# Threshold attention and a squared-ReLU network on one core: earlier loads for the third pair, an own order for attention's last two periods, and the last stores of the hidden layer asked for by ScalarE

## The chip, the core and the metric

One NeuronCore of a Trainium2 chip runs the whole program: TensorE (PE, the matrix engine), VectorE (DVE), ScalarE (ACT), GpSimd (POOL) and SyncE (SP), each with an instruction stream of its own, which it works off in order. The engines meet through semaphores. SP does no arithmetic: it asks for DMA transfers. ACT can ask for transfers too, as one more instruction of its own stream. The metric is the device time of one execution in microseconds (us), lower is better.

## The reference, cut to what matters

```python
# q, k, v: 8 batches x 8 heads x 576 x 64, fp32
scores = scale * np.matmul(q, k.transpose(0, 1, 3, 2))
thresh = np.max(scores, axis=-1, keepdims=True) - tau
scores = np.where(scores >= thresh, scores, -1000000000.0)
scores = scores - np.max(scores, axis=-1, keepdims=True)
attn = np.exp(scores)
attn = attn / (np.sum(attn, axis=-1, keepdims=True) + 1e-09)
attn_out = np.matmul(attn, v)
# to 4608 tokens x 512
x = attn_out.transpose(0, 2, 1, 3).reshape(B * S, H * D)
h = np.maximum(x @ w_in, 0.0)        # w_in 512 x 2048
out = h * h @ w_out                  # w_out 2048 x 512
```

## The kernel before, in words

**Attention** works on 32 pairs of heads. A pair's 2 x 576 query rows are cut into units of 128 rows, and with them the kernel counts unit pairs, 0 to 71 (called m). The work is laid out in periods (72 and a few more to fill and drain the pipeline). Each period runs a list of step names, in `run_period`; a name with `-` behind it belongs to the period before, with `--` to the one before that. There are two general lists (`PLAIN` and `CONVERTING`; the latter with steps that convert a chunk of the weights of `w_in`), and `BEGIN_WITH` holds lists of their own for periods 0 and 1. The order of the names is the order in which each engine gets its instructions.

The steps that matter here:

- `T` turns a pair's queries or keys on PE (transposes, L422) into `sc`, the tile of six PSUM banks.
- `SA`, `SB`, `RA`, `RB` are the score products (L458); `top`, `least`, `pow`, `mask`, `over` and `inv` are the softmax with its threshold, on DVE (L476, L491), POOL (L483) and ACT (L486).
- `V`, `W`, `U` turn the weights of one unit pair on PE (L402): `V` the first four of nine chunks of keys, `W` the fifth, `U` the last four. `V` and `U` write to `pt`, a PSUM place of two banks, which only one of them can hold at a time; `W` writes to banks 2 and 3 of `sc`. `Q` spreads the sums of the rows (L541) into what is left of `W`'s banks.
- `eV`, `eW`, `eU` copy the results to SBUF, by ACT (L549, in `filled`).
- `PV` multiplies the values with the turned weights over nine chunks of keys (L558), into banks 0 and 5; `x` takes the result out by ACT (L689) and DVE (L691), and `xm` scales one half on POOL (L701) and gives it to a store (L604).

Which instruction waits for which is worked out from the tiles; within `sc` the function `touch` tells the scheduler that accesses to different banks do not depend on one another, except for the pairs of kinds that `MEET` names, which do share data through SBUF.

**Loads at the start.** All are asked for by SP, in program order. `load_k` yields the key loads of a pair one by one, and last the two parts of `rn` (the 577th to 640th place of the turning: the last keys, L327, and the last queries, L328). The steps `ahead` and `more` ask for up to five such loads each. `load_v` (L337) loads a pair's values; the main loop calls it after periods 0, 1 and 2 for pairs 0, 1 and 2, and later ones follow when a place comes free. L194 loads chunks of `w_in`, which come as 64-bit numbers and are converted on ACT (L208), POOL and DVE for the hidden layer.

**The hidden layer** multiplies x with `w_in` by a scheme of seven products in place of eight, two levels deep. It runs in passes over blocks of tokens: the last is pass n = 8. In a pass the outer products come in the order `OUTER` = 1, 2, 6, 7, 4, 5, 3 (called m), and in each the inner products in the order 1, 6, 7, 5, 2, 4, 3 (`inner`, matmuls at L799). After inner product 1 ACT copies it from PSUM (L794): `copy(p1, X)`. Product 2 goes on in the same bank, so it needs that copy done. The other sums of a group are made by `final` and `sum_v` on DVE and POOL (L122, L125), some with another copy by ACT (L838).

The results of groups 2, 4, 5 and 3 are squared, four tiles each, by two ACT instructions (L951 and L952, in `square`), six inner products or more later; right behind them SP stores the tile to `g` in DRAM (L955 in pass 8). So pass 8 has 16 such stores of 256 KB.

**The output layer** reads `g` back (L1064) and multiplies it with `w_out` in the same scheme (also L799, the tile then is called `po`), in 9 steps of 49 products of 0.87 us. Its weights were prepared and put to DRAM earlier. In pass 8, while the hidden layer's weights leave `wall` one by one, `reload` (L1207) loads the 49 weights of the output layer into their places, 39 in the pass and 10 in the first output step, all by SP. In SP's order they stand between the stores of L955.

**Transfers.** In the program as built each DMA takes one of eight semaphores, in turn over the whole program and whatever engine asks for it. Before it is asked for, its engine waits until the DMA that took the same semaphore before, eight places back in program order, has landed. That wait stands in the stream of the engine that asks.

Of the kernel before, what the change touches and what calls it, by code (L numbers as in the profile page):

```python
# [48 lines left out]
def kernel(  # L49
# [25 lines left out]
    nc = tc.nc  # L75
# [5 lines left out]
    FULL = S // P  # L81
# [3 lines left out]
    BANK = 512  # L85
    MAIN = FULL * P
    STEP = 512
    NSTEP = B * S // STEP
# [202 lines left out]
    NU = len(units)  # L291
# [80 lines left out]
    behind = mybir.DependencyInfo(mybir.DependencyClass.Sync, mybir.DependencyReason.DATA)  # L372

    Q_RING, K_RING, W_RING = 3, 4, 2
    MEET = (("scores", "turnedq", (Q_RING,)), ("scores", "turnedk", (K_RING,)), ("last scores", "turnedk", (K_RING,)), ("values", "weights", (W_RING,)), ("x", "weights", (W_RING,)))

    def touch(what, made, at, size, key=0):

# [26 lines left out]
    def whole(pt, slot, count):  # L405

        return pt[:, :, ds(slot * HALF, count * HALF)].rearrange("p r (t q) -> p r t q", q=HALF)

    def joined(to):

        return to.rearrange("p (t r q) -> p r t q", r=2, q=HALF)
# [111 lines left out]
    def fill(m, f, pt, at=None):  # L523

        first, count = FILLS[f]
        if m not in wT:
            wT[m] = sb.tile([P, (2 * CH + 2) * P], FP32, tag="wT", bufs=W_RING, name="wT")
        for i, (u, c) in enumerate(FIRST[first : first + count]):
            half_turn(pt, i, weights[2 * m + u][:, c, :, :].rearrange("p j d -> p (j d)"), at)
# [11 lines left out]
                    made = nc.tensor.matmul(to, wide, ident[rows, rows], start=True, stop=True)  # L541
                    touch("turns", made, at + r * BANK, BANK)

    def filled(m, f, pt, at=None):

        first, count = FILLS[f]
        count += 2 * (f == "W")
        to = wT[m][:, ds(weight_at(first) * P, count * P)]
        touch("weights", nc.scalar.copy(joined(to), whole(pt, 0, count)), at, 2 * BANK, m)  # L549

    def values(m):

        for c in range(CH):
            for u in range(2):
                for s, (i, _, count, row) in enumerate(halves(2 * m + u)):
                    for j in range(2):
                        rows = ds(j * D, D)
                        made = nc.tensor.matmul(  # L558
                            sc[ds(u * D, D), ds(5 * j * BANK + row, count)], loaded_v[i][rows, (c - (u != j)) % CH, :],
                            wT[m][rows, ds(weight_at(2 * c + u) * P + row, count)],  # L560
                            start=(c == 0 and s == 0), stop=(c == CH - 1), skip_group_check=True,
                        )
                        touch("values", made, 5 * j * BANK, BANK, m)

    def valued(m):

# [18 lines left out]
    def has(n):  # L585
        return 0 <= n < NU
# [5 lines left out]
    def sums_due(p):  # L592

        return p > max(starts) + 2 and not converts(p)
# [43 lines left out]
        """.split(),  # L638
    }

    def spots():
        return [(sc[:, ds(b * BANK + REST, (FULL + 1) * HALF)], b * BANK) for b in (1, 4)]

    def middle():
        return sc[:, 2 * BANK : 4 * BANK].rearrange("p (r n) -> p r n", r=2)

    def period(p):

# [2 lines left out]
        late, pt = {"W": []}, {}  # L651

        def fills(f, m):
            if has(2 * m):
                pt[f] = pt_pool.tile([P, 2, BANK], FP32, tag="pt", name="pt")
                fill(m, f, pt[f])

        def evict(f, m):
            if has(2 * m):
                filled(m, f, pt[f], 2 * BANK if f == "W" else None)  # L660

        def W():
            if has(2 * m + 2):
                pt["W"] = middle()
                fill(m + 1, "W", pt["W"], 2 * BANK)

        def Q():
            if has(2 * m + 2):
                spread_sums(m + 1, pt["W"], 2 * BANK)

        def turn_some():
            free = None
# [42 lines left out]
        def every(key):  # L715
# [10 lines left out]
            "c1": lambda: convert1(begun(p)), "c2": lambda: convert2(begun(p)),  # L726
            "c3": lambda: convert3(begun(p)), "c4": lambda: convert4(begun(p - 1)),
            "c5": lambda: convert5(begun(p - 1)), "c6": lambda: convert6(begun(p - 1)),
            "s1": lambda: sums_due(p) and sums_step(), "s2": lambda: sums_due(p) and p < 60 and sums_step(), "ahead": lambda: ahead(5), "more": lambda: ahead(5),
            "fetch": lambda: (fetch(begun(p + 2)), fetch(begun(p + 3)) if p > 1 else None), "put": put, "give": lambda: ask(False),  # L730
        }
        steps["over"] = lambda: do(a, "over")
# [216 lines left out]
    def square(n, j, o):  # L949

        nc.scalar.activation(out=o, in_=o, func=AF.Relu)  # L951
        nc.scalar.activation(out=o, in_=o, func=AF.Square)  # L952
        steps, h = n
        if h is None:
            nc.sync.dma_start(out=gT[steps[0]][j][:, :].rearrange("p (k t) -> p k t", k=4), in_=o)  # L955
            return
        for s_, step in enumerate(steps):
            nc.sync.dma_start(
                out=gT[step][j][:, ds(h * BANK // 2, BANK // 2)].rearrange("p (k t) -> p k t", k=2),
                in_=o.rearrange("p (k s) t -> p k s t", s=2)[:, :, s_, :],  # L960
            )
# [199 lines left out]
    with tc.manual_schedule():  # L1161
        with ExitStack() as stack:
# [24 lines left out]
            turn(0, 1, spots(), nc.vector.tensor_copy)()  # L1187
            for p in range(FIRST_PERIOD, NU // 2 + 6):
                run_period(p)
                if 0 <= p < 3:  # L1190
                    load_v(p)
                if X_FIRST <= p < X_FIRST + 4:
                    load_x(0, XPARTS[p - X_FIRST :][:1])
                if p == X_FIRST + 4:
                    summing.append(prepare_x(0, lambda op, out, x, y: op(nc.gpsimd, out, x, y)))
# [191 lines left out]
```

## Time and profile before

| | us |
|---|---|
| time, median of 3 runs | 1281.78 (1280.94 to 1283.04) |
| the profiled execution | 1281.21 |
| its span in the trace | 1279.1 |
| PE busy | 1252.5 (98%) |
| DVE busy | 987.5 (77%) |
| POOL busy | 982.4 (77%) |
| ACT busy | 845.6 (66%) |

The profile is of one execution. Attention takes it to about 495.9 us from its start, the hidden layer to about 883.0, the output layer the rest. The granted clock of PE is nearly full over the whole span. A row of the waits says which engine and operation stood, what it waited for, and then the sum in us, how often, and the longest. A row of the timeline gives start and length in us, engine, line, operation, output and inputs, and in brackets how long the engine stood before and what ended that.

### The profile page before, as it was taken

The numbers are of one execution on the slowest core, as the hardware profiler recorded it, in microseconds if no ns is written. First come the engines' busy times: TensorE is split into PE (matmuls) and PEld (weight loads), VectorE is DVE, ScalarE is ACT, GpSimd is POOL, SyncE is SP. The second block draws the span as 40 slices with busy tenths as digits, with TensorE's granted clock in tenths as the row PEclk, the third lists the DMA queues.
The fourth block names the chain that finished last, engine by engine and source line by source line (L and its number), as shares of the span: only waits on it lengthen the run. The fifth ranks groups of instructions, "written<-read, shape, count | busy, mean of one in ns | idle before, by whom it ended". The sixth has DMA issues, their size and how long they took to land.

```text
span 1279.1 us, 55422 instructions
## 1 busy us (share of the span) xinstructions
PE 1252.5 (98%) x22991; PEld 1093.8 (86%) x22991; DVE 987.5 (77%) x2384; ACT 845.6 (66%) x1537; POOL 982.4 (77%) x1070
## 2 busy tenths in 40 slices
PE   7999999999999999999999999999999999999998
PEld 5777777777777778988888888999999999999998
DVE  6999999999999995886887877876646654665563
ACT  6999999999999994665765857665424432433240
POOL 2899898877776542987897989858777877787776
PEclk9999999999999999999999999999999999999999
DMA  7566667434333323658767868589654235523511
GB/s 185 131 170 149 176 191 195 117 93 104 85 86 86 80 58 84 203 170 232 209 190 215 229 169 239 164 304 361 240 164 162 65 109 167 167 57 112 167 35 35
DMA packets 291450, 196.81 MB, mean 154 GB/s; under 512 B 100096, under 2 KB 252160, under 8 KB 291200
## 3 DMA queue, kind: packets, MB, share of 16 engines
q1 hardware_dynamic: 289888, 192.87, 52.6%
q8 instruction: 181, 2.97, 1.0%
q14 instruction: 69, 0.57, 0.2%
q10 hardware_dynamic: 1312, 0.41, 0.1%
HBM read 120.85 MB, written 72.35 MB: 151 GB/s over the span
## 4 chain that ended last, share of the span: by engine, by line
PE 74%; DMA 2%; DVE 2%; ACT 1%; issue 1%; SPq 0%; POOL 0%; DVEq 0%; POOLq 0%; ACTq 0%
PE po L799 27%; PE ph L982 18%; PE ph L799 10%; PE sc L558 7%; PE sc L458 6%; PE pt L402 4%; PE sc L541 1%; PE sc L422 1%; DVE arena L125 1%; DMA arena<-g 1%; ACT c L838 1%; PE sc L402 0%; DMA wall<-w 0%; DVE arena L122 0%; ACT arena L951 0%
## 5 line engine op out<-in xcount | busy, mean ns | idle before, releaser
L125 POOL TENSOR_TENSOR arena<-arena 128x512 f32<-128x512 f32 (+1 forms) x314 | 378.3, 1224 | 130.5 <-DVE arena L125 118.7
L799 PE MATMUL po<-wall,arena 128*64 128x128 f32 x7056 | 388.3, 273 | 4.2 <-ACT arena L794 2.8
L799 PEld LDWEIGHTS po<-wall,arena 128*64 128x64 f32 x7056 | 386.7, 137 | 5.6 <-ACT arena L794 3.8
L125 DVE TENSOR_TENSOR arena<-ph,arena 128x512 f32<-128x512 f32 x378 | 254.8, 689 | 79.9 <-PE ph L982 31.9
L122 POOL TENSOR_TENSOR arena<-arena 128x128 f32<-128x128 f32 (+1 forms) x322 | 265.6, 826 | 23.8 <-DMA arena<-w 8.2
L982 PE MATMUL ph<-arena,wall 128*128 128x256 f32 x1176 | 256.6, 380 | 1.6 <-DVE arena L125 1.3
L982 PEld LDWEIGHTS ph<-arena,wall 128*128 128x128 f32 x1176 | 222.1, 190 | 36.0 <-DVE arena L125 5.8
L125 DVE TENSOR_TENSOR arena<-po,arena 128x128 f32<-128x128 f32 x378 | 108.0, 289 | 160.6 <-PE po L799 156.8
L491 DVE SCALAR_TENSOR_TENSOR arena<-arena 128x576 f32<-128x576 f32 x288 | 226.0, 821 | 0.0
L486 ACT ACTIVATE arena<-arena 128x576 f32<-128x576 f32 x288 | 213.3, 778 | 13.2 <-DVE arena L476 13.1
L476 DVE TENSOR_SCALAR_CACHE_REDUCE arena<-sc 128x576 f32<-128x576 f32 x288 | 203.3, 753 | 18.8 <-issue 7.7
L838 ACT COPY c<-arena 128x512 f32<-128x512 f32 (+1 forms) x295 | 169.0, 578 | 72.9 <-DVE arena L122 35.5
L458 PE MATMUL sc<-arena 64*64 64x512 f32 (+1 forms) x2304 | 178.8, 415 | 5.6 <-ACT arena L549 1.0
L558 PE MATMUL sc<-arena 64*64 64x128 f32 (+1 forms) x5760 | 165.9, 261 | 1.3 <-ACT arena L549 0.8
L122 DVE TENSOR_TENSOR arena<-arena,c 128x512 f32<-128x512 f32 x235 | 154.4, 666 | 12.7 <-ACT c L838 8.3
L558 PEld LDWEIGHTS sc<-arena 64*64 64x64 f32 x5760 | 150.7, 133 | 4.9 <-issue 1.0
L549 ACT COPY arena<-pt 128x1024 f32<-128x1024 f32 x144 | 145.7, 1012 | 3.8 <-PE pt L402 3.2
L458 PEld LDWEIGHTS sc<-arena 64*64 64x64 f32 x2304 | 76.7, 134 | 70.8 <-issue 46.5
L794 ACT COPY arena<-po 128x128 f32<-128x128 f32 x63 | 16.6, 263 | 181.8 <-PE po L799 177.0
L799 PE MATMUL ph<-arena,wall 128*64 128x128 f32 x2352 | 129.2, 273 | 0.6 <-DVE arena L691 0.6
L799 PEld LDWEIGHTS ph<-arena,wall 128*64 128x64 f32 x2352 | 128.3, 137 | 1.4 <-issue 1.0
L483 POOL TENSOR_SCALAR arena<-arena,tau_p 128x2 f32<-128x2 f32 x144 | 83.7, 581 | 57.9 <-DVE arena L476 43.5
(54 smaller groups left out, 1139.6 us busy)
## 6 DMA issues: line engine op xcount, KB each, us to landing
arena<-g SPq DMA_DIRECT2D x144, 256.0 KB, 5.1
g<-arena SPq DMA_DIRECT2D x192, 128.0 KB, 2.9
w<-arena SPq DMA_DIRECT2D x60, 256.0 KB, 3.0
wall<-w SPq DMA_DIRECT2D x49, 256.0 KB, 5.5
g<-arena SPq DMA_DIRECT2D x48, 256.0 KB, 3.7
arena<-w SPq DMA_DIRECT2D x44, 256.0 KB, 3.4
arena<-in_v_dram SPq DMA_DIRECT2D x32, 288.0 KB, 3.8
out_dram<-arena SPq DMA_DIRECT2D x70, 128.0 KB, 2.9
```

What stands on the lines that cost most here:

```text
L122: e.tensor_tensor(out=out, in0=x, in1=y, op=ALU.subtract)
L125: e.tensor_tensor(out=out, in0=x, in1=y, op=ALU.add)
L458: made = nc.tensor.matmul(sc[at, ds(to, count)], lhs, kT[rows, ds(at_k, count)], start=True, stop=True)
L476: made = nc.vector.tensor_scalar(out=s[:, j, :], in0=sc[:, ds(at, S)], scalar1=1.0, scalar2=None, op0=ALU.mult, op1=ALU.min, accum_out=nmx ...
L483: nc.gpsimd.tensor_scalar(out=thr, in0=nmx, scalar1=tau_p[:, :], scalar2=None, op0=ALU.add)
L486: nc.scalar.activation(out=w[:, :, j, :], in_=of(j), func=AF.Exp, bias=nmx[:, j : j + 1], scale=-1.0)
L491: nc.vector.scalar_tensor_tensor(out=w[:, :, j, :], in0=of(j), scalar=thr[:, j : j + 1], in1=w[:, :, j, :], op0=ALU.is_le, op1=ALU.mult, a ...
L549: touch("weights", nc.scalar.copy(joined(to), whole(pt, 0, count)), at, 2 * BANK, m)
L558: made = nc.tensor.matmul(sc[ds(u * D, D), ds(5 * j * BANK + row, count)], loaded_v[i][rows, (c - (u != j)) % CH, :], wT[m][rows, ds(weigh ...
L799: nc.tensor.matmul(to[cols], lhs[:, cols], rhs, start=start, stop=stop, skip_group_check=True)
L838: nc.scalar.copy(c, y)
L982: nc.tensor.matmul(to[:, 2 * j : 2 * j + 2, :], W_IN[m, k][:, ts(2 * h + j, P)], part_x(steps, k, m), start=(not more and j == 0), stop=Tr ...
```

## The change

It has three parts.

**A.** `load_v` is called after periods 0, 2 and 3 (for pairs 0, 1, 2 as before), and the step `more` asks for up to seven loads of keys and queries instead of five. On SP the two parts of `rn` of the third pair so come directly behind its keys, ahead of the second pair's values and of two chunks of `w_in`.

**B.** Period 73, the last but one that has work, gets its own list, which holds the steps of what is left of both last periods. On PE the values of unit pair 70 now stand before `V` of unit pair 71, where they stood behind it. For unit pair 71 `W` is put into banks 1 and 2, `U` into banks 3 and 4 of `sc` and not into `pt`, and `U` is copied out by DVE instead of ACT. Its values product is told as three kinds, so that only the last four chunks wait for `U`'s copy. POOL's order does not change.

**C.** The 16 stores of pass 8 (`steps[0] == NSTEP - 1`) are asked for by ACT, each right behind its second squaring instruction. SP then has 49 reloads in a row. In ACT's stream from the group m = 5 on stand, in order: copy of product 1 (m = 5), square and store four times, copy of product 1 (m = 3), and then squares and stores with copies of L838 between. (In program order the first of these four stores comes eight places behind the 22nd reload, the second behind the 25th, the third behind the 29th.)

```diff
--- before.py
+++ after.py
@@ -372,7 +372,7 @@
     behind = mybir.DependencyInfo(mybir.DependencyClass.Sync, mybir.DependencyReason.DATA)
 
     Q_RING, K_RING, W_RING = 3, 4, 2
-    MEET = (("scores", "turnedq", (Q_RING,)), ("scores", "turnedk", (K_RING,)), ("last scores", "turnedk", (K_RING,)), ("values", "weights", (W_RING,)), ("x", "weights", (W_RING,)))
+    MEET = (("scores", "turnedq", (Q_RING,)), ("scores", "turnedk", (K_RING,)), ("last scores", "turnedk", (K_RING,)), ("values", "weights", (W_RING,)), ("last values", "last weights", (W_RING,)), ("x", "weights", (W_RING,)))
 
     def touch(what, made, at, size, key=0):
 
@@ -541,12 +541,14 @@
                     made = nc.tensor.matmul(to, wide, ident[rows, rows], start=True, stop=True)
                     touch("turns", made, at + r * BANK, BANK)
 
-    def filled(m, f, pt, at=None):
+    def filled(m, f, pt, at=None, last=False):
 
         first, count = FILLS[f]
         count += 2 * (f == "W")
         to = wT[m][:, ds(weight_at(first) * P, count * P)]
-        touch("weights", nc.scalar.copy(joined(to), whole(pt, 0, count)), at, 2 * BANK, m)
+        copy_by = nc.vector.tensor_copy if last else nc.scalar.copy
+        kind = "last weights" if last else "weights"
+        touch(kind, copy_by(joined(to), whole(pt, 0, count)), at, 2 * BANK, m)
 
     def values(m):
 
@@ -560,7 +562,8 @@
                             wT[m][rows, ds(weight_at(2 * c + u) * P + row, count)],
                             start=(c == 0 and s == 0), stop=(c == CH - 1), skip_group_check=True,
                         )
-                        touch("values", made, 5 * j * BANK, BANK, m)
+                        part = "first values" if c < FULL else "values" if c == FULL else "last values"
+                        touch(part, made, 5 * j * BANK, BANK, m)
 
     def valued(m):
 
@@ -638,11 +641,21 @@
         """.split(),
     }
 
+    BEGIN_WITH[NU // 2 + 1] = """
+        give eU-- powA0-- V-- powA1-- eV-- maskA1-- PV-- powB1-- powB0-- maskA0-- U- W-- Q-- x--
+        maskB1-- maskB0-- eW-- over- inv- eU- xm-- PV- x- V- eV- W- Q- eW- xm- U eU PV x xm
+        """.split()
+
     def spots():
         return [(sc[:, ds(b * BANK + REST, (FULL + 1) * HALF)], b * BANK) for b in (1, 4)]
 
-    def middle():
-        return sc[:, 2 * BANK : 4 * BANK].rearrange("p (r n) -> p r n", r=2)
+    LAST = NU // 2 - 1
+
+    def w_bank(m):
+        return 1 if m == LAST else 2
+
+    def two_banks(first):
+        return sc[:, ds(first * BANK, 2 * BANK)].rearrange("p (r n) -> p r n", r=2)
 
     def period(p):
 
@@ -651,22 +664,27 @@
         late, pt = {"W": []}, {}
 
         def fills(f, m):
-            if has(2 * m):
+            if (f, m) == ("U", LAST):
+                pt[f] = two_banks(3)
+                fill(m, f, pt[f], 3 * BANK)
+            elif has(2 * m):
                 pt[f] = pt_pool.tile([P, 2, BANK], FP32, tag="pt", name="pt")
                 fill(m, f, pt[f])
 
         def evict(f, m):
-            if has(2 * m):
-                filled(m, f, pt[f], 2 * BANK if f == "W" else None)
+            if (f, m) == ("U", LAST):
+                filled(m, f, pt[f], 3 * BANK, True)
+            elif has(2 * m):
+                filled(m, f, pt[f], w_bank(m) * BANK if f == "W" else None)
 
         def W():
             if has(2 * m + 2):
-                pt["W"] = middle()
-                fill(m + 1, "W", pt["W"], 2 * BANK)
+                pt["W"] = two_banks(w_bank(m + 1))
+                fill(m + 1, "W", pt["W"], w_bank(m + 1) * BANK)
 
         def Q():
             if has(2 * m + 2):
-                spread_sums(m + 1, pt["W"], 2 * BANK)
+                spread_sums(m + 1, pt["W"], w_bank(m + 1) * BANK)
 
         def turn_some():
             free = None
@@ -726,7 +744,7 @@
             "c1": lambda: convert1(begun(p)), "c2": lambda: convert2(begun(p)),
             "c3": lambda: convert3(begun(p)), "c4": lambda: convert4(begun(p - 1)),
             "c5": lambda: convert5(begun(p - 1)), "c6": lambda: convert6(begun(p - 1)),
-            "s1": lambda: sums_due(p) and sums_step(), "s2": lambda: sums_due(p) and p < 60 and sums_step(), "ahead": lambda: ahead(5), "more": lambda: ahead(5),
+            "s1": lambda: sums_due(p) and sums_step(), "s2": lambda: sums_due(p) and p < 60 and sums_step(), "ahead": lambda: ahead(5), "more": lambda: ahead(7),
             "fetch": lambda: (fetch(begun(p + 2)), fetch(begun(p + 3)) if p > 1 else None), "put": put, "give": lambda: ask(False),
         }
         steps["over"] = lambda: do(a, "over")
@@ -952,7 +970,8 @@
         nc.scalar.activation(out=o, in_=o, func=AF.Square)
         steps, h = n
         if h is None:
-            nc.sync.dma_start(out=gT[steps[0]][j][:, :].rearrange("p (k t) -> p k t", k=4), in_=o)
+            queue = nc.scalar if steps[0] == NSTEP - 1 else nc.sync
+            queue.dma_start(out=gT[steps[0]][j][:, :].rearrange("p (k t) -> p k t", k=4), in_=o)
             return
         for s_, step in enumerate(steps):
             nc.sync.dma_start(
@@ -1187,8 +1206,8 @@
             turn(0, 1, spots(), nc.vector.tensor_copy)()
             for p in range(FIRST_PERIOD, NU // 2 + 6):
                 run_period(p)
-                if 0 <= p < 3:
-                    load_v(p)
+                if p in (0, 2, 3):
+                    load_v(max(p - 1, 0))
                 if X_FIRST <= p < X_FIRST + 4:
                     load_x(0, XPARTS[p - X_FIRST :][:1])
                 if p == X_FIRST + 4:
```

Line numbers in the changed kernel move: L549 is 551, L558 is 560, L604 is 607, L607 is 610, L689 and L691 are 707 and 709, L794 is 812, L838 is 856, L951 and L952 are 969 and 970, L955 is 974, L1064 is 1083, L1207 is 1226; what stands ahead of L549 keeps its number.

## The prediction

> **What bounds the kernel now.** I read the busy line first, then TensorE's waits, then a timeline round each wait that the change touches.
>
> ```profile
> PE 1252.5 (98%) x22991; PEld 1093.8 (86%) x22991; DVE 987.5 (77%) x2384; ACT 845.6 (66%) x1537; POOL 982.4 (77%) x1070
> ```
>
> ```profile
> PE po L799 <- ACT arena L794: 2.8, 1, 2.8
> ...
> PE pt L402 <- ACT arena L549: 1.7, 1, 1.7
> PE sc L422 <- DMA arena<-in_q_dram: 1.6, 1, 1.6
> ```
>
> TensorE (PE) works 98% of the span, so time can only come from its few stops. Each part of the change has one: 2.8 us where the output layer takes over (last layer, part C), 1.7 us where attention ends (part B), 1.6 us at the third pair's turning (part A). The change moves no arithmetic but one copy; I price it stop by stop, and look for stops that it makes.
>
> **Part A: the third pair's keys first.** PE's timeline; then a window behind the stop (length, busy time of PE, PEld, DVE, ACT and POOL, granted clock, DMA share, GB/s); then VectorE's timeline:
>
> ```profile
> 23.49 2.14 PE L558 MATMUL sc<-arena 64*64 64x128 f32 x72
> ...
> 26.12 0.41 PE L422 MATMUL sc<-ident,arena 64*128 64x64 f32 x8
> 28.15 0.34 PE L422 MATMUL sc<-ident,arena 64*128 64x64 f32 x2 [1.62 <-DMA arena<-in_q_dram]
> ...
> 31.49 2.08 PE L458 MATMUL sc<-arena 64*64 64x512 f32 x16
> 33.40 2.14 PE L558 MATMUL sc<-arena 64*64 64x128 f32 x72
> ...
> 39.34 1.20 PE L458 MATMUL sc<-arena 64*64 64x512 f32 x16
> 40.36 2.15 PE L558 MATMUL sc<-arena 64*64 64x128 f32 x72
> ```
>
> ```profile
> 30.00:33.40 3.40, 3.40 (x48) 1.96 (x49) 2.66 (x8) 2.38 (x4) 2.03 (x3) 0.51 0.23 49
> ```
>
> ```profile
> 29.74 0.76 DVE L476 TENSOR_SCALAR_CACHE_REDUCE arena<-sc 128x576 f32<-128x576 f32 x1 [2.67 <-issue]
> ```
>
> The last two of ten turnings wait 1.62 for the rows `rn` (L327, L328). Behind the stop the granted clock is 0.51, and 16 score products take 2.08 in place of 1.20. From one values product to the next (23.49 to 33.40) pass 9.91 us, in the next period 6.96.
>
> ```profile
> L328 SPq DMA_DIRECT2D arena<-in_q_dram x1: 602/602/602, 21.8 to 21.8; - x1
> ...
> DMA to landing us min/median/max: 6.3/6.3/6.3
> ```
>
> ```profile
> L337 SPq DMA_DIRECT2D arena<-in_v_dram x1: 606/606/606, 19.2 to 19.2; - x1
> ...
> DMA to landing us min/median/max: 3.6/3.6/3.6
> ```
>
> Now L327 and L328 are asked for right behind the pair's keys, ahead of the values' load of 19.2 and two weight chunks: L327 at about 19.2, L328 one issue (0.6) later, at 19.8. It lands between 23.4 (3.6 later) and 26.1 (6.3 later); its turning is due at 26.12 + 0.41 = 26.5. Both ends are in time, so the stop goes. What is moved back has room: the second pair's values are asked for at about 25, some 6 us later, and first used by the values product of 40.36; the weight chunks passed by feed only the weights of the next layer. What is late next is the engines of the softmax: VectorE (DVE) had 2.67 idle in this period, and rows of the next period show 6.96 with every engine in step. The gain is 9.91 - 6.96 = 2.95. Ends: only the stop itself, 1.6, if the half clock comes anyway; 1.62 and what 3.40 us at 0.51 lose, 1.67, together 3.3. I take **-2.9**, as the row of the whole next period has it.
>
> The Trainium skill, "TensorE: Matmul & The Clock Gate" (section "What's actually happening"), lets the clock fall to half only after at least one idle window of about 3.4 us. This trace disagrees: after a stop of 1.62 the clock is 0.51. By that rule the stop is not what halves the clock, and A would be worth 1.6; I carry that as a rival below.
>
> **Part B: order of the last two periods.** PE and ScalarE (ACT), each from its own timeline:
>
> ```profile
> 488.23 0.71 PE L402 MATMUL pt<-ident,arena 64*128 64x64 f32 x16 [1.68 <-ACT arena L549]
> 488.87 2.20 PE L558 MATMUL sc<-arena 64*64 64x128 f32 x72
> ...
> 492.97 2.33 PE L558 MATMUL sc<-arena 64*64 64x128 f32 x108 [0.75 <-ACT arena L549]
> 495.87 4.37 PE L799 MATMUL ph<-arena,wall 128*64 128x128 f32 x76 [0.57 <-DVE arena L691]
> ```
>
> ```profile
> 487.16 1.02 ACT L549 COPY arena<-pt 128x1024 f32<-128x1024 f32 x1
> ...
> 492.81 1.02 ACT L549 COPY arena<-pt 128x1024 f32<-128x1024 f32 x1
> ```
>
> Before: V of unit pair 71 (0.71) waits until ACT has emptied the transposes' bank (487.16 + 1.02 = 488.18), then values 70 (2.20), U, W, sums, values 71 (2.33). After: values 70 start at 486.55, five ninths of them (1.22) need nothing of that copy; the rest waits for 488.18 and ends at about 489.2. V 71 takes to 489.8, ACT's copy of it to 490.9, W and the sums (0.29 + 0.46) to 490.6, U (0.71, in the score banks) to 491.3, and values 71 start at once. Their last four ninths need U's copy, now on DVE. A copy of 1024 by DVE is not in the trace: from below, ACT's 1.02; from above, DVE's 0.76 for 576 (the row of 29.74) scaled to 1024, 1.35. I take 1.2, between the two, which lie close; it ends at 492.5, while PE is in the first five ninths (1.29) until 492.6. So the copy is hidden; at 1.35 it shows 0.1. Values 71 end at 493.65, and with the same 0.57 the hidden layer starts at 494.2 in place of 495.87: **-1.65**, ends -1.2 (the copy and its wake-up late) and -2.1 (values 70 found ready earlier).
>
> **Part C: the last 16 stores of g by ACT.** Rows of ACT, PE and DVE round the handover:
>
> ```profile
> 873.03 0.63 ACT L952 ACTIVATE arena<-arena 128x512 f32<-128x512 f32 x1
> ...
> 878.00 0.58 ACT L794 COPY arena<-ph 128x512 f32<-128x512 f32 x1 [0.79 <-PE ph L799]
> ...
> 889.18 0.27 ACT L794 COPY arena<-po 128x128 f32<-128x128 f32 x1 [4.81 <-POOL arena L125]
> ```
>
> ```profile
> 883.02 3.66 PE L799 MATMUL po<-wall,arena 128*64 128x128 f32 x64
> 889.50 35.21 PE L799 MATMUL po<-wall,arena 128*64 128x128 f32 x592 [2.81 <-ACT arena L794]
> ```
>
> ```profile
> 884.64 0.69 DVE L125 TENSOR_TENSOR arena<-ph,arena 128x512 f32<-128x512 f32 x1 [2.99 <-DMA g<-arena]
> ```
>
> The old stop: DVE waits 2.99 for a g store to land (it reuses the store's buffer); POOL's sums and ACT's copy follow, PE stands 2.81. The store was late since it stood in SP's queue behind reloads of `wall`. With ACT asking, that queue is left. But in the program as built each DMA takes the next of eight semaphores and is asked for only when the DMA eight places back in program order has landed:
>
> ```profile
> SPq L1207 <- DMA wall<-w: 6.1, 18, 0.9
> SPq L955 <- DMA wall<-w: 3.8, 9, 1.1
> ```
>
> These two rows are that wait: a reload and a store each held by a reload into other memory. On SP it holds transfers alone. On ACT it holds every square and every copy behind it, for which PE waits. The reloads stay on SP, eight under way with the DMA engines full:
>
> ```profile
> 860.00:880.00 20.00, 20.00 (x372) 20.00 (x370) 16.02 (x25) 9.75 (x18) 17.29 (x15) 1.00 1.00 350
> 880.00:900.00 20.00, 17.19 (x286) 16.95 (x283) 12.15 (x26) 12.53 (x25) 14.35 (x12) 0.91 1.04 382
> ```
>
> ```profile
> L1207 SPq DMA_DIRECT2D wall<-w x1: 319/319/319, 873.3 to 873.3; - x1
> ...
> DMA to landing us min/median/max: 5.9/5.9/5.9
> ```
>
> ```profile
> L1207 SPq DMA_DIRECT2D wall<-w x1: 1087/1087/1087, 880.0 to 880.0; - x1
> ...
> DMA to landing us min/median/max: 5.2/5.2/5.2
> ```
>
> So the chain after is this. The store behind the square of 873.03 (done 873.66) is eight places behind the reload of 873.3: it goes out at 873.3 + 5.9 = 879.2, and ACT stands 5.5. The third store of the four is eight behind the reload of 880.0: out at 885.2, having let two squares by in between. An issue costs ACT about 0.35 (SP's 0.32 rows); with it and two activations of 0.63 the fourth store is out at 886.85, then ACT makes the copy that it made at 878.00, done at 887.8. PE needs that copy for the fourth of the seven products of the group, at 878.0 + 3 x 0.87 = 880.5: it stops **7.35**. Two more stops in that group: a DVE sum behind the copy, 0.4; a C copy (L838) behind two more activations and a store, 1.25. The output layer starts at 883.02 + 9.0 = 892.0, its first 3.66 end at 895.7. The old stop there does not go: ACT's second C copy, behind another store, ends at 893.8; before, 4.5 us passed from DVE's release (884.64) to the copy of 889.18, and less one DVE sum of 0.69 that is done by then, 3.85 pass now: 897.65. PE goes on at 898.0 in place of 889.50, which is **+8.5**.
>
> Elsewhere: the first four stores of the pass, earlier on, stop ACT in the same way and PE some 2 us; nothing is added, as the 879.2 and 885.2 above are set by the reloads and not by PE. Four later stores lie among ACT's slack. SP is free of the stores and costs nothing.
>
> The unknown is how soon a store asked by ACT lands, as later stores stand on earlier ones. The trace has two transfers on ACT's queue late in the kernel (the landing is that of all four of their line):
>
> ```profile
> L1107 ACTq DMA_DIRECT2D out_dram<-arena x2: 575/605/635, 1274.1 to 1275.4; - x2
> ...
> DMA to landing us min/median/max: 2.1/2.2/2.2
> ```
>
> Ends: 2.2 with the engines idle, 5.2 like SP's reloads in the same microseconds. I take 3, the row of ACT's own queue and one transfer's share more. At 5.2 two later stores come out 1.5 us later each, so +11.5; at 2.2 C stays at +8, since the reloads rule.
>
> The Trainium skill, "DMA: Bandwidth & Descriptors" (section "Queues, rings and completion order"), says that a DMA engine takes turns between the queues that have work, packet by packet. No run here shows it yet. By it a store on ACT's queue does not stand behind SP's eight reloads, and the sum is that with 3; without it, that with 5.2.
>
> **Sum.** -2.9 - 1.65 + 8.5 = +3.95. On the profiled execution's 1281.21 that is 1285.2; the median of the runs lies 0.57 above that execution, so **1285.7 us**.
>
> **Rivals.**
> - *Reloads land a little earlier.* Four stores of 0.66 each no longer stand ahead of them on SP: 879.2 becomes 876.6, and a store lands in 2.2. C falls to about +5.5: 1281.78 - 4.55 + 5.5 = 1282.7. Against it: the engines are full, and the stores still go through them.
> - *The semaphores do not bite (faster).* Reload and square cross at one point: had the reload of 873.3 landed before 873.7, 5.5 us earlier, ACT would never stand, stores would go out with their squares, and up to 2.8 of the old stop would go. Half of that for the 16 issues: C -1.4, 1275.8. For it: SP is free of stores. Against it: DMA share 1.00, so 5.5 us is eight transfers too many.
> - *A store on ACT lands like SP's.* C +11.5: 1288.7.
> - *The half clock does not go with the stop of part A*, as by the page above: A -1.6, 1287.0.
> - *The start does not gain*, another transfer being late in the place of `rn`: A 0, 1288.6.
>
> **How the numbers follow.** Forecast 0.38 (its own range 1283 to 1288), earlier reloads 0.23, semaphores that do not bite 0.14, ACT's stores slow 0.11, half clock stays 0.08, start without gain 0.06. A measurement of this kernel tells about 0.2%, 2.6 us, from no change: same is 1279.2 to 1284.3. Faster: 0.14 and 0.02 from the earlier reloads, 0.16. Same: 0.21 of these and 0.03 of the forecast, 0.24. Slower: 0.60. The range reaches from 1280 (reloads still earlier) to 1291 (slow stores with the half clock on top, and 1 for the four later stores); what lies outside is the faster rival and a few hundredths.
>
> **What would show it.** A: no wait at L422, no clock of 0.5 between 30 and 33, second distance of values products near 7. B: hidden layer's first product about 1.6 earlier than A alone sets it. C: on ACT, stops ahead of stores that end with reloads' landings; PE stops of about 7 us inside the last hidden group; output layer's start later by 9 against the hidden layer's start. Wrong would make it: ACT without such stops, or a C that shows in ACT but not in PE.

## The result and the profile after

The changed kernel takes 1288.69 us (median of 5 runs, 1286.13 to 1289.96) against 1281.15 (5 runs, 1280.52 to 1283.04): the ratio is 1.0054, with a 95% interval of 1.0040 to 1.0069. It is slower by 7.5 us. The profiled execution took 1288.88 us with a span of 1287.1, 8.0 over the span of before.

The busy line and TensorE's waits, after:

```profile
PE 1255.0 (98%) x22991; PEld 1096.9 (85%) x22991; DVE 989.4 (77%) x2385; ACT 846.2 (66%) x1536; POOL 981.0 (76%) x1070
```

```profile
PE po L817 <- ACT arena L812: 5.4, 3, 3.1
PE ph L817 <- ACT arena L812: 4.3, 2, 2.5
```

The old waits of parts A and B (1.6 at L422, 1.7 at L402) are no longer at the head. In their place stand waits for ACT's copy of product 1 (L812) in the hidden layer's last pass, 4.3, and a longer sum of them in the output layer, 5.4 for 2.8.

Where the 8 us arise is seen by cutting the span at fixed products. Every kernel here has 22,991 matmul records, and those at the cuts are the same products in each. The table gives the time from one cut to the next, in us:

| kernel (profiled execution) | start to the 12,001st | to the hidden layer's first | to the 15,501st | to the 15,601st | to the 15,881st | to the output layer's first | to its 65th | to the end of TensorE's last |
|---|---|---|---|---|---|---|---|---|
| before | 479.70 | 16.17 | 363.36 | 5.46 | 15.28 | 3.05 | 6.47 | 386.00 |
| after (A, B, C) | 478.90 | 14.49 | 364.46 | 9.60 | 15.28 | 7.82 | 6.80 | 386.09 |
| A alone | 474.84 | 16.17 | 363.49 | 5.46 | 15.28 | 3.05 | 4.43 | 384.58 |
| B alone | 482.23 | 14.49 | 362.97 | 5.46 | 15.28 | 3.05 | 6.49 | 384.39 |
| C alone | 479.20 | 16.17 | 363.53 | 11.41 | 15.28 | 7.60 | 6.27 | 385.28 |
| A and B | 475.81 | 14.49 | 363.03 | 5.46 | 15.28 | 3.05 | 4.43 | 384.56 |
| first four stores by ACT | 484.02 | 16.17 | 366.00 | 11.14 | 15.65 | 3.05 | 4.43 | 384.51 |
| A, B, later reloads | 478.44 | 14.49 | 368.51 | 5.46 | 15.28 | 3.05 | 4.43 | 390.15 |
| A, B, C, later reloads | 479.28 | 14.49 | 366.09 | 8.18 | 15.28 | 8.84 | 5.00 | 387.74 |
| last twelve by ACT | 479.78 | 16.18 | 367.77 | 5.46 | 15.28 | 7.27 | 7.43 | 384.90 |
| C, small reloads | 476.37 | 16.18 | 363.19 | 9.82 | 15.65 | 4.36 | 5.83 | 384.97 |
| small reloads | 479.47 | 16.17 | 363.58 | 5.46 | 15.28 | 3.05 | 4.43 | 384.66 |
| A, B, stores by POOL | 475.45 | 14.49 | 364.51 | 5.46 | 15.28 | 3.05 | 8.23 | 385.92 |
| A, B, four stores by POOL | 476.39 | 14.48 | 362.36 | 5.46 | 15.28 | 3.05 | 6.35 | 385.60 |

Part A gained 0.80 in this execution, part B 1.68, a stretch that no part touches lost 1.10, and C lost 4.14 + 4.77 + 0.33 = 9.24 in three stretches; with 0.1 at the end the sum is 8.0.

The rows behind it, TensorE's timeline after, first at the start:

```profile
26.82 0.66 PE L422 MATMUL sc<-ident,arena 64*128 64x64 f32 x10
27.41 1.20 PE L458 MATMUL sc<-arena 64*64 64x512 f32 x16
```

All ten turnings now stand in one row without a stop (the load L328 was asked for at 19.56 and took 2.7), and the score products behind them are at full clock, 1.20. Then the end of attention, PE and DVE:

```profile
487.44 1.10 PE L560 MATMUL sc<-arena 64*64 64x128 f32 x32 [0.47 <-ACT arena L551]
...
490.34 2.48 PE L560 MATMUL sc<-arena 64*64 64x128 f32 x108
493.39 2.84 PE L817 MATMUL ph<-arena,wall 128*64 128x128 f32 x48 [0.57 <-DVE arena L709]
```

```profile
490.38 1.23 DVE L551 COPY arena<-sc 128x1024 f32<-128x1024 f32 x1 [1.40 <-PE sc L402]
```

The stop of 1.68 is 0.47, that of 0.75 is gone: U's copy on DVE (1.23) lies beside the values product. And the last pass:

```profile
863.32 20.02 PE L817 MATMUL ph<-arena,wall 128*64 128x128 f32 x336 [2.46 <-ACT arena L812]
885.20 1.09 PE L817 MATMUL ph<-arena,wall 128*64 128x128 f32 x16 [1.86 <-ACT arena L812]
886.72 1.91 PE L817 MATMUL ph<-arena,wall 128*64 128x128 f32 x16 [0.43 <-DVE arena L125]
889.08 1.64 PE L817 MATMUL ph<-arena,wall 128*64 128x128 f32 x16 [0.45 <-DVE arena L125]
890.56 3.66 PE L817 MATMUL po<-wall,arena 128*64 128x128 f32 x64
897.36 7.84 PE L817 MATMUL po<-wall,arena 128*64 128x128 f32 x112 [3.14 <-ACT arena L812]
```

```profile
863.00:867.00 4.00, 3.68 (x40) 3.65 (x42) 3.76 (x7) 1.38 (x3) 1.22 (x1) 0.58 1.04 395
884.00:892.00 8.00, 5.92 (x76) 5.29 (x78) 3.27 (x5) 4.78 (x8) 2.90 (x3) 0.79 1.04 392
```

(The second fence is a table of windows; the third number from the right is the granted clock.) Two new stops, 2.46 and 1.86, with half clock behind them; the stop at the output layer's 65th product is 3.14, where it was 2.81. ACT's own timeline tells who stands for whom:

```profile
875.80 0.63 ACT L970 ACTIVATE arena<-arena 128x512 f32<-128x512 f32 x1
876.46 0.34 ACTq L974 DMA_DIRECT2D g<-arena  x1
876.84 0.63 ACT L969 ACTIVATE arena<-arena 128x512 f32<-128x512 f32 x1 [0.41 <-ACT arena L970]
877.50 0.63 ACT L970 ACTIVATE arena<-arena 128x512 f32<-128x512 f32 x1
878.42 0.33 ACTq L974 DMA_DIRECT2D g<-arena  x1
878.79 0.63 ACT L969 ACTIVATE arena<-arena 128x512 f32<-128x512 f32 x1 [0.65 <-DMA wall<-w]
879.45 0.63 ACT L970 ACTIVATE arena<-arena 128x512 f32<-128x512 f32 x1
881.74 0.33 ACTq L974 DMA_DIRECT2D g<-arena  x1
882.11 0.63 ACT L969 ACTIVATE arena<-arena 128x512 f32<-128x512 f32 x1 [2.03 <-POOL arena L125]
882.78 0.63 ACT L970 ACTIVATE arena<-arena 128x512 f32<-128x512 f32 x1
884.14 0.33 ACTq L974 DMA_DIRECT2D g<-arena  x1
884.56 0.59 ACT L812 COPY arena<-ph 128x512 f32<-128x512 f32 x1 [1.15 <-DMA g<-arena]
```

The squares themselves take 1.3 each; between them ACT stands, and the copy for which PE stops at 885.20 is made at 884.56. Where the row names POOL, the store at 881.74 is what came just before, and it was asked for when the reload eight places back had landed: that reload was asked for at 876.41 and took 5.3, as the first below; the store of 876.46 in the same way stands on the reload of 869.67, the second below. The third fence is that of the twelve stores between 853 and 896. The store of 884.14, the last ahead of that copy, stands on no reload: eight places back is the store that ACT itself asked for at 878.42, and the row names `g`. In the program as built, five of the 16 stores stand behind a reload, seven behind an earlier store of ACT's own, and four behind loads and stores of `g` that SP asked for.

```profile
L1226 SPq DMA_DIRECT2D wall<-w x1: 383/383/383, 876.4 to 876.4; - x1
...
DMA to landing us min/median/max: 5.3/5.3/5.3
```

```profile
L1226 SPq DMA_DIRECT2D wall<-w x1: 1223/1223/1223, 869.7 to 869.7; - x1
...
DMA to landing us min/median/max: 6.7/6.7/6.7
```

```profile
L974 ACTq DMA_DIRECT2D g<-arena x12: 326/326/337, 854.0 to 895.0; - x12
...
DMA to landing us min/median/max: 4.9/5.3/5.8
```

The first new stop, ahead of 863.32, ends in the same way. On ACT's timeline the store of 861.80 went out when ACT's own store of 856.47, eight places back, had landed, and the copy that PE needs came behind it:

```profile
862.16 0.59 ACT L856 COPY c<-arena 128x512 f32<-128x512 f32 x1 [1.19 <-DMA g<-arena]
862.69 0.58 ACT L812 COPY arena<-ph 128x512 f32<-128x512 f32 x1
```

### The profile page after: what moved, and what is told of

Same layout as the page of the kernel before. It is cut to its first block, busy times and chain, and to the rows that moved or that the text cites. A ratio compares the mean times of both kernels' runs of the same rounds, so it can differ in the third digit from the quotient of the medians.

```text
span 1287.1 us, 55425 instructions
## 1 busy us (share of the span) xinstructions
PE 1255.0 (98%) x22991; PEld 1096.9 (85%) x22991; DVE 989.4 (77%) x2385; ACT 846.2 (66%) x1536; POOL 981.0 (76%) x1070
## 4 chain that ended last, share of the span: by engine, by line
PE 71%; DMA 5%; ACT 2%; DVE 1%; issue 1%; SPq 1%; POOL 0%; ACTq 0%; DVEq 0%; POOLq 0%
PE po L817 30%; PE ph L1001 16%; PE ph L817 7%; PE sc L560 7%; PE sc L458 6%; PE pt L402 3%; DMA wall<-w 2%; DMA g<-arena 1%; PE sc L541 1%; PE sc L422 1%; DMA arena<-xT 1%; DVE arena L125 1%; ACT arena L969 1%; DMA arena<-g 1%; ACT c L856 0%
## 5 line engine op out<-in xcount | busy, mean ns | idle before, releaser
L817 PE MATMUL ph<-arena,wall 128*64 128x128 f32 x2352 | 132.9, 276 | 5.8 <-ACT arena L812 4.3
L817 PEld LDWEIGHTS ph<-arena,wall 128*64 128x64 f32 x2352 | 130.9, 139 | 7.8 <-ACT arena L812 4.8
L812 ACT COPY arena<-po 128x128 f32<-128x128 f32 x63 | 16.6, 264 | 180.8 <-PE po L817 177.7
```

Of the source, the lines that this page charges most:

```text
L817: nc.tensor.matmul(to[cols], lhs[:, cols], rhs, start=start, stop=stop, skip_group_check=True)
```

## The experiments

The theory: C's loss is what ACT stands, ahead of each store, until the transfer eight places back has landed. Its rivals: the earlier start that A and B give makes the meeting of stores and reloads; the time ACT spends on asking, and the new order of its work; or crowding of the transfers. The runs were made in three groups, the first and the third on one chip and the second on another, and the time of before differs between the groups (1277.33, 1282.01 and 1278.81 us), so each run is compared with the runs of before in its own group; a difference in us is the ratio's, taken of the median of before.

**A alone**

```diff
-  "more": lambda: ahead(5)
+  "more": lambda: ahead(7)
-                if 0 <= p < 3:
-                    load_v(p)
+                if p in (0, 2, 3):
+                    load_v(max(p - 1, 0))
```

> Only part A: the loads at the start. Theory (the gain at the start is real, 2 us at 45 us, but attention's small stops give it back, as the changed kernel's products came level with before at about 193 us): the values products near 45 us stand 2 us earlier than before, the end of attention less than 1 earlier, time 0 to 1 us under before. Rival (the give-back in the profiled execution was chance, or came from the other parts): the end stays 2 to 3 us under before.

Measured: ratio 0.9983 (0.9962 to 1.0003), unclear, with equal medians (1277.31 and 1277.33). In its profile the gain was not given back: 4.9 at the 12,001st product against the profile of before shown above, which is of another group. The start of the kernel varies from run to run: over the seven profiles with A that product stands at 474.8 to 479.3, mean 477.0; over the seven without at 476.4 to 484.0, mean 480.1. The difference of the means, 3.1, is near what was forecast, but with this scatter it is uncertain by some 2.5; the changed kernel's own 0.8 lies at the poor end. The stop that A removes varies too. In the seven profiles without A it is 1.62 (before), 3.46, 1.92, 1.98 and 1.02, and in two there is none; with A there is none in all seven. Where it was above 1.6, the 601st product stands at 41.6 to 44.0 us; in the other three without A at 39.1 to 39.6, and with A at 38.0 to 39.5. So A takes away a stop that only some executions have. Neither expectation is borne out as it stands: the end had moved more than the theory allowed, and the times can't tell it from 0.

**B alone**

```diff
+    BEGIN_WITH[NU // 2 + 1] = """ ... """     # with banks, kinds and DVE's copy as in the change
```

> Only part B: order of the last two periods. Theory: the hidden layer starts 1.8 us earlier against the period before it, and part of that is lost at the hidden layer's wait near 605 us, which a load of x ends; time 0.5 to 1.8 us under before. Rival (the wait near 605 is no fixed time): the whole 1.8 stays.

Measured: ratio 0.9978 (0.9956 to 1.0000), 2.8 us less with an interval that ends at 0. The stretch from the 12,001st product to the hidden layer's first is 14.48 or 14.49 in each profile with B and 16.17 or 16.18 in each without: 1.68, to a hundredth. The stretch behind it is 362.97, not longer than before's 363.36, so the wait near 605 us that took 1.1 in the changed kernel's profile doesn't belong to B. The rival was right.

**C alone**

```diff
-            nc.sync.dma_start(out=gT[steps[0]][j]...
+            queue = nc.scalar if steps[0] == NSTEP - 1 else nc.sync
+            queue.dma_start(out=gT[steps[0]][j]...
```

> Only part C: the last 16 stores asked for by ScalarE. Theory (ScalarE stands before each store until the transfer eight places back has landed, and TensorE behind it): 8 to 10 us over before, all between 855 and 915 us. Rival (the earlier start of the last pass, by A and B, is what brought stores and reloads together): 5 us over before or less.

Measured: 1289.62 us, ratio 1.0087 (1.0055 to 1.0119), 11 us over before by the ratio. The three stretches lose 5.95, 4.55 and -0.20. So C needs neither A nor B for its loss.

**A and B, stores by SP**

> Parts A and B, with the stores asked for by SyncE as before. Theory (C is the whole loss): 1 to 2.6 us under before, with the old stop of about 2.8 at the first output products. Rival (parts interact, A and B alone bring the stop of the handover forward): as before or slower.

Measured: 1274.56 us, ratio 0.9963 (0.9942 to 0.9984), 4.7 us under before by the ratio (interval 2.0 to 7.4; 2.8 by the medians), the lowest ratio of this study, though its interval overlaps that of B alone. The gain expected, 1 to 2.6, is not excluded. The old stop at the output layer's 65th product, expected to stay, had shrunk, PE's timeline:

```profile
881.56 12.67 PE L817 MATMUL po<-wall,arena 128*64 128x128 f32 x224 [0.77 <-ACT arena L812]
```

The same 0.77 stands in the profile of A alone and of others on which SP asks for the stores, while before and B alone have 2.8. What decides between the two was not settled. In the profile of A and B the transfers were quicker (378 to 397 GB/s between 840 and 880 us against 320 to 366 in before), which would bring the stores out sooner. A alone (376 to 394) and B alone (306 to 376, with the old stop) fit that; it was not tried by itself.

**Reloads asked for later, with A and B, and with all three parts**

```diff
-                if 7 * i + at > 9:
-                    reload(7 * i + at - 10)
+                if 7 * i + at > 23:
+                    reload(7 * i + at - 24)
-                if n == 0 and 7 * i + at < 10:
-                    reload(39 + 7 * i + at)
+                if n == 0 and 7 * i + at < 24:
+                    reload(25 + 7 * i + at)
```

> Parts A and B, stores asked for by SyncE, and each reload asked for 14 products later than before (24 products behind the start of the last pass in place of 10). Theory (stores come late since SyncE's queue is full of reloads): stores go out within 1 us of their squares, the first output products no longer stop for 2 us, time 1 to 3 us under that of A and B alone. Rival (the stop has another cause, or the reloads are late for the output layer's first weights): the same as A and B, or stops of the output layer on wall.

> All three parts, and each reload asked for 14 products later. Theory (ScalarE stands since the transfer eight places back, mostly a reload, has not landed, as the reloads run behind): the transfer eight places back is then 5 products old and has landed, ScalarE stands little, and C's loss falls from 9 to 3 us or less against the same kernel with SyncE's stores. Rival (asking costs ScalarE its time, 16 issues of 0.35 and their order, whatever the reloads do): C's loss stays over 5 us.

Measured: ratios 1.0009 (0.9989 to 1.0028) and 1.0059 (1.0038 to 1.0081). These two are no test of the theory. In the built program of the second, 40 of the 49 reloads still stand in a row where they stood, and the first nine ACT stores stand eight places behind the same transfers as in the changed kernel: the scheduler, not the place in the text, orders the reloads. The two stretches lost 2.72 and 5.79 in place of 4.14 and 4.77. The time itself, 6.4 us over the first kernel by the ratios, is what the rival of the second named; but with the order unchanged the theory gives such a loss as well. The first kernel got two new stops near 923 us (2.3 and 1.7), so later reloads are no gift either.

**The first four stores alone, and the last twelve alone**

```diff
+            first = j in (5, 0, 4, 1)       # the group of outer product 2
+            queue = nc.scalar if steps[0] == NSTEP - 1 and first else nc.sync
```

> Before, with the first four of the 16 stores (the group of outer product 2) asked for by ScalarE. Theory (what the changed kernel's trace shows at 863 us, a stop of 2.5 and half clock behind it, is a loss of its own): 2 to 5 us over before. Rival (as the prediction had it, later stops that the reloads set take it up): 1 us over before or less.

> Before, with the last twelve stores asked for by ScalarE, the first four by SyncE. Theory (each group of stores stops TensorE by itself): 5 to 8 us over before, with no stop near 863. Rival (the reloads' landings set the end alone): as much as part C by itself, 9 us or more, since TensorE comes earlier and waits as long for the same landings.

Measured: the first four 1.0023 (1.0004 to 1.0041), 2.9 us over before; the last twelve (with `not first`) 1.0053 (1.0037 to 1.0069), 6.8 us. PE's timelines, the first four, then the last twelve:

```profile
872.16 24.05 PE L799 MATMUL ph<-arena,wall 128*64 128x128 f32 x384 [2.96 <-ACT arena L794]
```

```profile
886.19 1.09 PE L799 MATMUL ph<-arena,wall 128*64 128x128 f32 x16 [1.13 <-ACT arena L794]
887.72 1.09 PE L799 MATMUL ph<-arena,wall 128*64 128x128 f32 x16 [0.43 <-DVE arena L125]
890.24 1.71 PE L799 MATMUL ph<-arena,wall 128*64 128x128 f32 x16 [1.43 <-DVE arena L125]
```

Each group loses in its own stretch and leaves the other at its old 5.46 and 3.05. The two losses add up (9.7 us, C alone 11 in another group). Nothing later takes up the first stop: the theory was right for both runs.

**The stores asked for by POOL (all 16, and four)**

```diff
-            queue = nc.scalar if steps[0] == NSTEP - 1 else nc.sync
+            queue = nc.gpsimd if steps[0] == NSTEP - 1 else nc.sync
```

(The second kernel: only for `j in (13, 8, 12, 9)`.) In the built program these transfers take semaphores of their own, and only two of the 16 wait for one of them.

> The changed kernel with the 16 stores asked for by GpSimd (POOL) in place of ScalarE. GpSimd's transfers have semaphores of their own in the program as built, so none waits for a reload. Theory (C costs what ScalarE stands for the transfers eight places back): ScalarE does not stand, the stops of TensorE near 863 and 885 go, time 3 us under before or better, as A and B alone or up to 2 us under that, as the stores no longer stand behind reloads; POOL's own cost of asking may take 1 or 2 of it. Rival (the stores, asked for among the reloads by whatever engine, crowd the transfers): a loss of over 4 us stays.

> Parts A and B, with four of the 16 stores, those of outer product 4 (g 13, 8, 12, 9), asked for by GpSimd and the other twelve by SyncE. Theory (the old stop comes from these four standing behind reloads on SyncE): the same time as with all 16 asked for by GpSimd or better, 0 to 2 us under A and B alone. Rival (POOL's asking delays its sums, on which the first output products wait as well): as A and B alone or slower.

Measured: 0.9990 (0.9974 to 1.0006) and 0.9988 (0.9972 to 1.0004), no change that could be told. With all 16, the two stretches in which ACT's stores cost 4.14 and 4.77 are back at 5.46 and 3.05 (see the table): the same stores at the same places, off SP, and no stop. So the rival of crowding, a loss of over 4 us by whatever engine, is out. But PE's and POOL's timelines show a new one:

```profile
886.47 15.30 PE L817 MATMUL po<-wall,arena 128*64 128x128 f32 x224 [4.57 <-ACT arena L812]
```

```profile
880.22 1.09 POOL L974 DMA_DIRECT2D g<-arena  x2
881.32 1.28 POOL L125 TENSOR_TENSOR arena<-arena 128x512 f32<-128x512 f32 x1
882.53 1.09 POOL L974 DMA_DIRECT2D g<-arena  x2
883.64 3.70 POOL L125 TENSOR_TENSOR arena<-arena 128x512 f32<-128x512 f32 x3
```

Asking costs POOL 0.55 each, ahead of the sums that the output layer's 65th product waits for (2.2 in these rows): 4.57 there in place of 0.77 with A and B. Four stores by POOL leave 2.69 there, as the rival of that run had it. So the theory holds for where ACT stood, and its forecast that the stores would be gained by it doesn't.

**Small reloads, without and with C**

```diff
-            nc.sync.dma_start(out=t[:, :], in_=w_dram[ds(at * P, P), :])
+            nc.sync.dma_start(out=t[:, 0:64], in_=w_dram[ds(at * P, P), 0:64])
```

> Before, with an eighth of each reload (64 of 512 columns of each of the 49 weight tiles; the rest of the tile is left as it was). It is the base for the next run. Theory (the old stop at the first output products comes from stores that stand behind 256 KB reloads): that stop of 2.8 shrinks to 1 or less, time 1 to 3 us under before. Rival: the stop stays.

> Part C alone, with an eighth of each reload as in the run before (the rest of the tile is left as it was). Order and number of ScalarE's instructions are as in C. Theory (ScalarE stands for landings that are late since the transfers are large): the landings come in time, C costs 3 us or less against the run before. Rival (16 issues on ScalarE, 0.35 each, and their order cost the 9 us): C costs 6 us or more against the run before.

These kernels load 64 of the 512 columns of each reload and leave the rest of the tile as it was, so their output is not that of the reference.

Measured: 0.9975 (0.9956 to 0.9995) without C. The stop at the 65th product is 0.77, as the theory said, but 0.77 also stands in profiles with full reloads, so this run doesn't show where the old stop came from. With C it is 1.0043 (1.0021 to 1.0065). C thus costs 8.7 us by the ratios and 6.3 by the medians (1283.81 and 1277.53); in the profiles its three stretches lose 4.36, 1.31 and 1.40, in sum 7.1. (The ends of the two profiles lie only 4.3 apart, as the start of the kernel, which C doesn't touch, was 3.1 quicker in the one with C.) That is more than the theory said: by the time alone the rival came out. ACT's timeline tells more:

```profile
875.96 0.63 ACT L952 ACTIVATE arena<-arena 128x512 f32<-128x512 f32 x1
876.62 0.33 ACTq L956 DMA_DIRECT2D g<-arena  x1
877.00 0.63 ACT L951 ACTIVATE arena<-arena 128x512 f32<-128x512 f32 x1 [0.40 <-POOL arena L125]
...
880.01 0.33 ACTq L956 DMA_DIRECT2D g<-arena  x1
880.43 0.59 ACT L794 COPY arena<-ph 128x512 f32<-128x512 f32 x1 [0.45 <-PE ph L799]
```

At the second place each store now stands behind a small reload, goes out behind its square and costs 0.40, nothing more, and the copy of product 1 is in time: that stretch loses 1.31 in place of 4.55. At the first place the loss stays, 4.36. Its third and fourth stores stand behind small reloads too and cost 0.40 each. The transfers eight places behind its first two are a load and a store of `g`, which keep their 256 KB, and ACT stands for them:

```profile
852.59 0.63 ACT L951 ACTIVATE arena<-arena 128x512 f32<-128x512 f32 x1 [0.77 <-DMA arena<-g]
...
855.78 0.59 ACT L838 COPY c<-arena 128x512 f32<-128x512 f32 x1 [1.90 <-DMA wall<-w]
```

(The second row names a reload that landed near that time; the store eight places back in the program is one of `g`, asked for by SP.)

So at the second place the run shows that most of the loss is the wait for landings. At the first place that is read from the rows, and was not varied. What 16 times 0.40 and the new order of ACT's work cost is the rest, 1.31 at the second place and up to 1.40 at the handover (5.83 against 4.43): the rival is part of the loss, not the whole.

## Why the prediction was right, and where it was not

The direction, and the reason for it, came out: A and B gain, C loses more, as ACT stands ahead of its stores for transfers that have not landed. The time lies in the range, 3.0 over the forecast, but above the forecast's own 1283 to 1288. It meets the figures of two rivals, 1288.7 (a store by ACT lands like SP's) and 1288.6 (the start does not gain), without either having come as it was worked out. By its steps:

- **A, -2.9:** the stop and the half clock behind it went, as worked out: from one values product to the next pass 7.20 us (24.21 to 31.41) in place of 9.91. At the 601st product 2.1 were gained (39.47 for 41.58), as the products ahead of this place came later in this execution: the granted clock was 0.50 over 16.5 to 23.2, where before had 0.75. At the end of attention 0.80 was left. Two small stops took most of the rest, 0.41 ahead of 60.79 and 0.77 ahead of 90.97. The second came in other profiles too, with A (0.44, 0.37, 0.72) and without (0.38, small reloads); the runs don't tell what sets them. What the forecast did not see is that the stop itself is not in every execution of a kernel without A, so that one profile can't give A's mean gain.
- **B, -1.65:** 1.68, with DVE's copy at 1.23 for the 1.2 taken. Right.
- **C, 8.5:** 9.24, but by other terms. The copy of product 1 was to stop PE by 7.35 and two sums by 1.65; the whole stretch lost 4.77. The step that was mis-sized is the landing of the reloads, taken from before's trace: freed of the stores ahead of it, SP had that reload landed at 876.4 in place of 879.2, and the other at 881.7 in place of 885.2. It was given as a rival, with 876.6. That the total came so near is luck: 4.14 that was put at nothing and 4.23 that did not come in the last group cancel.
- **The first four stores, "nothing is added":** wrong. That stretch lost 4.14 (a stop of 2.46, and half clock, 1.7) and never gave it back: the reason given, that the reloads alone set the end, failed in the run with the last twelve.
- **A store by ACT lands in 3:** it took 5.3, as long as SP's reloads (5.4, the median of all 49). The rival that had this set C at 11.5; it came without the reloads' late landing, and with 9.24. As stores stand on stores, it also reaches back into the last group: the store of 884.14 went out 5.7 after ACT's own of 878.42, when that had landed. The Trainium skill, "DMA: Bandwidth & Descriptors" (section "Queues, rings and completion order"), has the engines take turns between queues; here a store on ACT's nearly empty queue was no faster than one behind eight of SP's. By the section "Issuing engines are not separate DMA queues" of that page in the Trainium skill, asking from another engine saves only the time of asking; the landings here agree.
- **The half clock as the Trainium skill has it** ("TensorE: Matmul & The Clock Gate", section "What's actually happening") would have left A with 1.6. All ten turnings and the products behind them ran at full clock once the stop was gone, so for this stop the row was the better guide.
- **The handover, "the old stop does not go":** right, 3.14 for 2.81, though with SP's stores it went in several profiles, which the forecast had not seen as possible. What makes it come and go stays open.

The forecast was 4 us for the 8 that came: 2.1 of what is missing is A's in this execution, 0.7 is C's, and 1.1 is the hidden layer's, which varies by as much (362.4 to 368.5 in all profiles) and was in no part of the change.

## What to carry to other kernels

A transfer is not free for the engine that asks: where semaphores are shared in turn, it stands there until an older transfer has landed, and everything behind it on that engine stands with it. So put such requests on an engine that nothing waits for, and check which transfer stands the given number of places back. When several edits come together, time each alone: here two good ones, 4.7 us together (2.0 to 7.4), were hidden by the third. And look at a stop in several profiles of the same kernel before pricing it: the one of part A was 0 to 3.5 us.

## What the runs showed of the hardware

- Stops of TensorE of 2.46 and 1.86 us were followed by half clock (0.58 over 863 to 867, 0.79 over 884 to 892); the first cost 4.14 in all. Both are shorter than the idle window of about 3.4 us that the Trainium skill names ("TensorE: Matmul & The Clock Gate", section "What's actually happening"), as was the stop of 1.62 in before. But not every such stop was followed by it: after 2.31 us ahead of 604.15 in the changed kernel (clock 1.00 over 604.2 to 608) and after 2.83 ahead of 889.97 in B alone (1.00 over 890 to 894) it stayed full. So the length alone does not decide; what does was not tried.
- With SP's and ACT's transfers of 256 KB under way together (DMA share 1.02 and 1.04 in the windows of 860 to 900), the median from asking to landing was 5.4 us for SP's reloads and 5.3 for ACT's stores; with an eighth of the reloads' bytes a store by ACT took 2.0 to 3.5 in the same stretch.
- Asking costs ACT 0.33 (0.40 with the gap to its next instruction) and POOL 0.55.
